# Lightning attention and a routed expert layer on one core: the order of two weight requests, and the form of one step's score products

## The chip, the cores and the metric

The kernel runs on one core of one Trainium2 chip. The metric is the device time of one execution in microseconds (us); the time before is the median of four runs. The profile is that of one more execution, with the start and end of every instruction and the marks that transfers leave when they land.

## The reference

Two stages. The first is a block-wise causal attention with a decay per head; the second sends each token through one of eight experts.

```python
# q, k, v: (4, 8, 768, 64), block of 64, a decay lam per head
for b in range(nb):
    intra = einsum('bhic,bhjc->bhij', qb, kb) * Dmask      # lam**(i-j) for i >= j
    intra = einsum('bhij,bhjd->bhid', intra, vb)
    inter = einsum('bhid,bhde->bhie', qb * lam_pow, kv_state)
    out[:, :, sl] = intra + inter
    kv_state = lam_block * kv_state + einsum('bhsd,bhse->bhde', kb_dec, vb)
# x = out as (4, 768, 512); w_gate (512, 8), w1 (8, 512, 1024), w2 (8, 1024, 512)
for s in range(S):
    fresh_e = argmax(logits[b, s])
    e = fresh_e if s == 0 or local_gate[b, s] < 0.5 else prev_e
    h = maximum(x[b, s] @ w1[e], 0)
    out[b, s] = p[e] * (h @ w2[e])                         # p: softmax of the logits
```

All values are 32-bit floats. The expert of a token depends on the attention's output, so which weights are needed is known only while the kernel runs.

## The kernel before, in words

**Attention.** 24 steps, one for 128 positions of one sequence (`ORDER`, four sequences in turn). A step's input is loaded on SP's queue into one of six buffers. TensorE (PE) multiplies queries by keys (`scores`), VectorE (DVE) multiplies by the decay mask (L212), PE multiplies by the values (`mix`, L248) after the part from the state (`from_state`, L235), updates the state (`update`, L262) and turns the output to rows (`rows_of`, L272), which go to DRAM. `scores(s + 1)` runs ahead of `mix(s)` in steps 0 and from 6 on; in steps 1 to 4 it comes after it, and `scores(6)` comes between `from_state(5)` and `mix(5)`.

**Two forms of the score products.** A step has four pairs of heads, and `u` picks the head of a pair; a head has 64 channels, which are the rows of the product. For the steps in `WIDE` (3, 4, 5, 6) each head is one product of 128 keys by 128 queries (L200): 8 products. For the other steps the keys are cut in two halves of 64, and the second half is multiplied with the second 64 queries only (L208), since later keys are masked for earlier queries: 16 products. Both write the same PSUM banks; what the second form leaves unwritten has a zero in the mask.

**Experts.** While attention ends, the tokens are ranked by expert and cut into tiles of 128 rows of one expert. The first five tiles (0 to 4, `KA` = 5) use the tokens of the first half of the positions. The rest becomes pairs of tiles (two tiles of one expert, multiplied in a scheme of seven products instead of eight, with sums of the weights made on DVE), some whole tiles, and half tiles for what is left (the first of them a quarter tile here). In this run the order is: tiles 0 to 3; tile 4 and the preparation of the first pair; pairs 0 and 1 with three half tiles spread over them as hooks; pair 2; three whole tiles; the rest of the pairs.

**Weights.** There are three sets of buffers, each w1 (first layer) and w2 (second layer), 2 MB each: `w1t[0..2]`, `w2t[0..2]`. Tiles 0 to 3 and 4 alternate between sets 0 and 1. Pair 0 uses set 1, pair 1 set 0, the half tiles set 2. All weight transfers are issued by SP, on one queue, in the order in which the program names them. `weights_of(g, i, layers)` reads the expert of tile `g` into a register and issues the transfers of the layers into set `i` (L685 for w1, L687 for w2). A transfer is issued only when the last reader of its buffer is done, and what stands behind it in SP's order waits too.

**Around the change.** At the end of the first block SP's order is: pair 0's w1 (after tile 3's first layer, since tile 3 uses set 1), the first half tile's w1 and w2 (`G2`; w1 when `by_slots` has read what lay in `w1t[2]`; `w2t[2]` is free), then in the second block the three numbers that choose the branches, and pair 0's w2 (when tile 3's second layer has been multiplied). Next are the second pair's weights, asked for in hook 1 of pair 0 after a copy on DVE (L1204).

In pair 0 DVE makes the sums of w1 (`sums_1`, L935 and L936), adds up products (L993), makes the first sums of w2 (`sums_2`, L937), flips a gathered tile (L717) and adds two more products (L1003, L1004), in this order. PE's product into `c` (bank `po0`, L1011) needs L1004. The half tile's steps run in hooks 7 to 10 of pair 0: turned (L1086), first layer (L1096, reads `w1t[2]`), turned again (L1106), second layer (L1118, reads `w2t[2]`). The weights of the next half tile are asked for when these are done.

Both blocks run under a manual schedule: every engine's order is the program's.

Of the kernel before, what the change touches and what calls it, by code (L numbers as in the profile page):

```python
# [38 lines left out]
PARTS = [(0, 8), (8, NA), (NA, NT)]  # L39
LOADS = 6  # L40
QUARTERS = [16, 17, 18, 19]
WIDE = [3, 4, 5, 6]
WARM = 10
KA = -(-(NA * P - E * (P - 1)) // P)

# [8 lines left out]
G2 = G1 + E  # L54
# [10 lines left out]
def kernel(  # L65
# [26 lines left out]
    def w1_src(e):  # L92
        return w1[bass.ds(e, 1)].rearrange("o (t p) f -> p (o t) f", p=P)

    def w2_src(e):
        return w2[bass.ds(e, 1)].rearrange("o (t p) d -> p (o t) d", p=P)
# [89 lines left out]
    def scores(s):  # L186
# [8 lines left out]

        if s in WIDE:
            for a in range(A):
                for u in range(2):
                    rows = slice(DH * u, DH * u + DH)
                    nc.tensor.matmul(ps[u][:, a], lhsT=kt[rows, a], rhs=qt[rows, a],  # L200
                                     start=True, stop=True, skip_group_check=True)
        for a in range(A if s not in WIDE else 0):
            for j in range(2):
# [434 lines left out]
    def rows_out(i):  # L638

        got = nows["got"]  # L640
        nc.vector.tensor_scalar(got[:, 0], got[:, 0], 0.0, float(SKIP), ALU.is_equal, ALU.mult)
        nc.vector.tensor_tensor(sidx[i], got[:, 0], gidx[i], ALU.add)

    def both_halves():

        twin = pl[:, :5 * (E + 1)].rearrange("p (k g) -> p k g", k=5)
        few = nows["few"]
        nc.tensor.matmul(twin[:, :, :E], lhsT=dupb, rhs=few, start=True, stop=True, skip_group_check=True)
        nc.tensor.matmul(twin[:, :, E:], lhsT=dupq, rhs=few[:, :, 0:1], start=True, stop=True, skip_group_check=True)
        got = act.tile([P, 5, E + 1], F32, name="twin", bufs=1)  # L650
        nc.vector.tensor_copy(got, twin)
        src = act.tile([P, 2, E + 1], F32, name="srch", bufs=1)
        nc.vector.tensor_scalar(src[:, 0], got[:, 0], -float(P), 0.0, ALU.add, ALU.max)
        nc.vector.tensor_scalar(src[:, 1], got[:, 0], 0.0, float(SKIP), ALU.is_equal, ALU.mult)
        nc.vector.tensor_tensor(src[:, 0], src[:, 0], src[:, 1], ALU.add)
        nc.vector.tensor_tensor(src[:, 0], src[:, 0], got[:, 1], ALU.add)
        nc.vector.scalar_tensor_tensor(sidxh[:, :E], src[:, 0, :E], 2.0, upper.broadcast_to([P, E]), ALU.mult, ALU.add)
        nc.vector.scalar_tensor_tensor(sidxh[:, E:], src[:, 0, E:], 4.0, fourth, ALU.mult, ALU.add)
        nc.vector.tensor_tensor(got[:, 2], got[:, 2], got[:, 3], ALU.add)
        nc.vector.tensor_tensor(gateh, got[:, 2], got[:, 4], ALU.add)  # L660
# [7 lines left out]
    def expert(g, own=None):  # L668
        i, j = at(g)
        if own:  # L670
            i = own
        return nc.values_load(owner[i][0:1, j:j + 1], engines=[SP], min_val=0, max_val=E - 1,
                              skip_runtime_bounds_check_because="an index of 8 experts")
# [8 lines left out]
    def weights_of(g, i, layers=(1, 2), cond=None, own=None):  # L682
        e = expert(g, own)
        if 1 in layers:
            nc.sync.dma_start(out=w1t[i], in_=w1_src(e), cond=cond, cond_hint=None if cond is None else True)  # L685
        if 2 in layers:
            nc.sync.dma_start(out=w2t[i], in_=w2_src(e), cond=cond, cond_hint=None if cond is None else True)  # L687

    def w_of(p):
        return (p + 1) % 2  # L690
# [44 lines left out]
    def output(i, w, fs=range(FT)):  # L735
        for f in fs:
            nc.tensor.matmul(pys[i], lhsT=hq[f // 4, i][:, f % 4], rhs=w2t[w][:, f], start=(f == 0), stop=(f == FT - 1))  # L737
# [28 lines left out]
    def number(k, n):  # L766
        return nc.values_load(arms[k][0:1, 0:1], min_val=0, max_val=n - 1,
                              skip_runtime_bounds_check_because="a number of tiles")
# [16 lines left out]
    with tc.manual_schedule(engines={PE, DVE, SP, POOL}):  # L785
# [125 lines left out]
        weights_of(KA, w_of(0), (1,))  # L911
        output(1, 1, range(FT // 2))
        by_slots(1, (0, 1, 2, 3, 4))
        weights_of(G2, 2)
        output(1, 1, range(FT // 2, FT))
        written(3, 1)

# [47 lines left out]
    def pair_ahead(p):  # L965
        for i in range(2):
            ahead(KA + 2 * p + i, i)
# [212 lines left out]
    with tc.manual_schedule(engines={PE, DVE, SP, ACTE}):  # L1180
        more, fulls, halves = (number(k, n) for k, n in enumerate((PMAX - PMIN + 1, E + 1, FIRST_SMALL + 1)))
        weights_of(KA, w_of(0), (2,))
        both_halves()
        pair_ahead(0)
        rows_out(1)
        ahead_half(0)
        sums_1(0, range(3))
        pair_flipped(0)
        pair_flipped(1)
        hidden(0, 0, 0)  # L1190
        hidden(0, 0, 1)
        pair_moved(0, 0)
        moved(xp(0, 1), xqs[1], copy=nc.vector.tensor_copy)
        sums_1(0, (3,))
        output(0, 0)
        sums_of_x(0)
        pair_ahead(1)
        written(4, 0)

        def first_pairs(n, first=2):  # L1200
            hooks = hooks_of_halves(n, first)

            def loads():
                nc.vector.tensor_copy(owner[2], owner[1])  # L1204
                weights_of(KA + 2, w_of(1), own=2)

            hooks.setdefault(1, []).insert(0, loads)
            pair(0, hooks)
            pair(1, {k - 14: f for k, f in hooks.items()})

        def others():
            weights_of(G1, 2)
            rows = [xgh, *xgt]

            def full_ahead(f):
                collect(rows[f % 3], *at(G1 + f))

            pair(2, {0: [lambda: full_ahead(0)], 10: [lambda: full_ahead(1)], 12: [lambda: full_ahead(2)],
                     6: [lambda: flipped(xqs[0], rows[0])], 7: [lambda: moved(xtt[0], xqs[0])]}, load=False, further=False)

            def w_of_full(f):
                return w_of(2) if f % 2 else 2

            def full(f, n=E):

                i, w = f % 2, w_of_full(f)
                if f + 3 < n:
                    full_ahead(f + 3)
                if not f:
                    weights_of(G1 + 1, w_of_full(1), cond=fulls > 1)  # L1230
                if f + 1 < n:
                    flipped(xqs[1 - i], rows[(f + 1) % 3])
                hidden(i, w, 0)
                hidden(i, w, 1)
                if f + 1 < n:
                    moved(xtt[1 - i], xqs[1 - i])
                output(i, w)
                written(G1 + f, i)
                if f + 2 < n:
                    weights_of(G1 + f + 2, w, cond=fulls > f + 2)  # L1240

            def rest(asked=False):
                if not asked:
                    pair_ahead(4)
                weights_of(KA + 8, w_of(4), cond=more > 0)
                rows_of_pair(3)
                pair(3, cond=more > 1, write=False)

                def later_pair(k, last):

                    write_pair(yt)
                    pair(PMIN + k, {11: [lambda: rows_of_pair(PMIN + k)]}, next=not last, load=not last and PMIN + k + 2 < PMAX,
                         cond=more > k + 2, write=False)

                def later_pairs(k):

                    if PMIN + k + 1 == PMAX:
                        return later_pair(k, True)
                    with tc.If(more > k + 1, preferred_fallthrough_block=True) as cmp:
                        later_pair(k, False)  # L1260
                        later_pairs(k + 1)
                    with cmp.Else():
                        later_pair(k, True)

                with tc.If(more > 0, preferred_fallthrough_block=True) as cmp:
                    later_pairs(0)
                with cmp.Else():
                    for i in range(2):
                        nc.vector.tensor_copy(yl[:, i], yt[:, i])

            with tc.If(fulls == 3, preferred_fallthrough_block=True) as cmp:
                for f in range(3):
                    full(f, 3)
                    if f:
                        ahead(KA + 7 + f, f - 1)
                rest(True)
            with cmp.Else():
                while_more(fulls, 0, E, None, full)
                rest()


        with tc.If(halves == FIRST_SMALL, preferred_fallthrough_block=True, label="halves") as cmp:
            first_pairs(3, 4)
            others()
        with cmp.Else():
            one_of(halves, [3, 4, 2, 5, 1, 6, 0, 7, 8], None, first_pairs)
            others()
        write_pair(yl)
# [44 lines left out]
```

## Time and profile before

| what | us |
|---|---|
| four runs | 452.09, 452.58, 453.19, 458.5 |
| their median | 452.88 |
| the profiled execution | 450.47 |
| its span, first to last instruction | 448.7 |
| attention (to the first expert product) | 0 to 100.9 |
| tiles 0 to 4 | 100.9 to 176.6 |
| pairs 0 and 1 with the half tiles | 176.6 to 251.2 |
| pair 2, three whole tiles, the other pairs | 251.2 to 441.5 |

The granted TensorE clock is 0.998 on the mean. Weights and inputs come over the DMA queue q1 (104.62 MB). PE's rate of work in the 40 slices is 9 tenths nearly everywhere.

In the profile a line such as L937 is a line of the kernel; an arrow shows what is written from what is read; "x16" is the number of instructions. A 32-bit product appears as two matmul records, so the 8 products of L200 are 16 records and the 16 of L208 are 32 (some records merge in the views). The chain that ended last is read from the end backwards: each entry was released by the one before it.

The forms of the score products, from the answer for each line:

```profile
L200 PE MATMUL ps<-inp x64: 272/272/373, 15.8 to 28.7; 64*128 64x128 f32 x64
```
```profile
L208 PE MATMUL ps<-inp x608: 213/269/321, 6.5 to 95.6; 64*64 64x128 f32 x116, 64*64 64x64 f32 x36
```

These are times of one record from issue to modelled end in ns; records overlap.

### The profile page before, as it was taken

The page shows a single profiled execution, that of the slowest core. Times are in us where ns is not written, and L with a number is a line of the kernel's source. Part 1 is how long each engine was busy: PE and PEld are TensorE (multiplying, and loading weights), DVE is VectorE, ACT ScalarE, POOL GpSimd, SP SyncE. Part 2 cuts the span into 40 slices and gives each one's busy share as a digit, 9 for nine tenths or more (in the row PEclk, how much of TensorE's full clock was granted, in tenths as well). Part 3 has the DMA queues.
Part 4 walks back from the last instruction along what each step waited for, and adds up shares of the span by engine and source line. Part 5 has one row for each costly group of instructions (what it writes and reads, how often), then busy time and mean ns, then how long its engine had stood idle before and what let it go on. Part 6 is the DMA issues. An engine that isn't in the chain of part 4 may idle for free.

```text
span 448.7 us, 10497 instructions
## 1 busy us (share of the span) xinstructions
PE 432.6 (96%) x4186; PEld 359.3 (80%) x4186; DVE 278.3 (62%) x562; ACT 201.7 (45%) x594; POOL 109.3 (24%) x120
## 2 busy tenths in 40 slices
PE   7999999999999999699999999999999999999993
PEld 6887887778666786688686999677899999898982
DVE  5547777871339959666473796100487888878661
ACT  2356566446455105543534448451445455556110
POOL 4476565321100042103220400210102011020101
PEclk9999999999999999999999999999999999999999
DMA  8999999979899899999993599997153838380101
GB/s 271 408 421 403 317 315 347 383 250 368 304 400 362 277 406 380 355 404 383 380 362 127 172 403 367 349 354 271 43 212 104 309 103 284 138 282 4 53 3 51
DMA packets 42575, 124.85 MB, mean 278 GB/s; under 512 B 3148, under 2 KB 3148, under 8 KB 40592
## 3 DMA queue, kind: packets, MB, share of 16 engines
q1 hardware_dynamic: 34976, 104.62, 63.8%
q0 software_dynamic: 4368, 13.90, 8.9%
q10 hardware_dynamic: 3168, 5.51, 3.3%
q8 instruction: 37, 0.61, 0.5%
q14 instruction: 26, 0.21, 0.2%
HBM read 124.02 MB, written 12.91 MB: 305 GB/s over the span
## 4 chain that ended last, share of the span: by engine, by line
PE 76%; DMA 12%; issue 5%; DVE 4%; POOLq 0%; POOL 0%
PE ps L731 11%; PE pk L962 11%; PE pk L737 11%; PE ps L957 10%; DMA out_dram<-y,sidxp 6%; PE po L248 5%; DMA w<-in_w_dram 5%; PE po L957 5%; PE pl L962 4%; PE ps L208 3%; PE pk L272 3%; PE pk L262 2%; PE pr L1118 2%; PE po L235 2%; PE pr L1096 2%
## 5 line engine op out<-in xcount | busy, mean ns | idle before, releaser
L731 PEld LDWEIGHTS ps<-xt,w 128*128 128x128 f32 x512 | 58.2, 192 | 3.0 <-issue 2.9
L731 PE MATMUL ps<-xt,w 128*128 128x128 f32 x512 | 59.1, 276 | 0.3 <-issue 0.3
L737 PE MATMUL pk<-w,h 128*128 128x512 f32 x128 | 56.5, 593 | 0.0
L737 PEld LDWEIGHTS pk<-w,h 128*128 128x128 f32 x128 | 23.6, 190 | 26.3 <-issue 25.6
L703 POOL DMA_INDIRECT xg<-x_dram,gidx x25 | 25.8, 1032 | 60.5 <-DVE lg L717 39.3
L746 POOL DMA_INDIRECT out_dram<-y,sidx x14 | 14.0, 1002 | 105.8 <-DVE y L763 46.5
L212 DVE TENSOR_TENSOR sm<-ps,mask 128x512 f32<-128x512 f32 x46 | 29.6, 685 | 14.8 <-PE ps L200 7.4
L724 ACT COPY xp<-xlast 32x128 f32<-32x128 f32 x128 | 37.8, 295 | 1.7
L733 ACT ACTIVATE h<-ps 128x512 f32<-128x512 f32 x16 | 9.6, 597 | 57.6 <-PE ps L731 57.6
L724 ACT COPY xp<-lg 32x128 f32<-32x128 f32 x112 | 33.0, 295 | 2.6
L763 DVE TENSOR_SCALAR y<-pk,gate 128x512 f32<-128x512 f32 x8 | 6.0, 744 | 42.1 <-PE pk L737 30.4
L957 PEld LDWEIGHTS ps<-xp,w 128*128 128x128 f32 x256 | 30.5, 192 | 1.7 <-issue 1.3
L957 PE MATMUL ps<-xp,w 128*128 128x128 f32 x256 | 31.3, 275 | 0.0
L957 PE MATMUL ps<-xs,s 128*128 128x128 f32 x256 | 31.2, 275 | 0.0
L177 POOL TENSOR_TENSOR qd<-inp,lamq 128x512 f32<-128x512 f32 x20 | 25.6, 1278 | 22.4 <-PE po L235 10.6
L962 PE MATMUL pk<-w,h 128*128 128x256 f32 x128 | 30.5, 381 | 0.0
L962 PE MATMUL pk<-s,hsum 128*128 128x256 f32 x128 | 30.3, 380 | 0.0
L957 PEld LDWEIGHTS ps<-xs,s 128*128 128x128 f32 x256 | 29.9, 192 | 0.0
L248 PE MATMUL po<-sm,inp 128*64 128x128 f32 x384 | 27.7, 280 | 2.1 <-DVE sm L212 1.2
L248 PEld LDWEIGHTS po<-sm,inp 128*64 128x64 f32 x384 | 20.9, 136 | 9.1 <-issue 6.8
L962 PEld LDWEIGHTS pk<-s,hsum 128*128 128x128 f32 x128 | 23.9, 190 | 3.3 <-DVE s L1045 0.2
L962 PEld LDWEIGHTS pk<-w,h 128*128 128x128 f32 x128 | 23.5, 190 | 3.4 <-issue 0.6
(280 smaller groups left out, 793.1 us busy)
## 6 DMA issues: line engine op xcount, KB each, us to landing
w<-in_w_dram SPq DMA_DIRECT2D x43, 2048.0 KB, 9.9
inp<-in_qkv_dram SPq DMA_DIRECT2D x15, 1024.0 KB, 8.3
x_dram<-xn ACTq DMA_DIRECT2D x21, 256.0 KB, 3.1
inp<-in_qkv_dram SPq DMA_DIRECT2D x10, 512.0 KB, 8.8
inp<-in_qkv_dram SPq DMA_DIRECT2D x4, 768.0 KB, 6.9
w<-in_w_dram SPq DMA_DIRECT2D x4, 512.0 KB, 8.9
x_dram<-xn SPq DMA_DIRECT2D x2, 256.0 KB
xg<-x_dram,gidx POOLq DMA_INDIRECT x25
```

What stands on the lines that cost most here:

```text
L177: nc.gpsimd.tensor_tensor(qd, x[:, 0].rearrange("p (a i) -> p a i", i=P), lamq, ALU.mult)
L208: nc.tensor.matmul(ps[u][half, a, first:], lhsT=kt[rows, a, half], rhs=qt[rows, a, first:], start=True, stop=True, skip_group_check=True)
L212: nc.vector.tensor_tensor(sm[:, u], ps[u], mask[:, u], ALU.mult)
L248: nc.tensor.matmul(head(a, u), lhsT=vn[:, a, u], rhs=sm[:, u, a], start=(not c and a < 2), stop=True, skip_group_check=True)
L272: nc.tensor.transpose(px[:, P * a:P * a + P], xc[:, a, ORDER[s][0]], ident)
L703: nc.gpsimd.indirect_dma_start(out=xg, out_offset=None, in_=x_dram[:n, :], in_offset=bass.IndirectOffsetOnAxis(ap=gidx[i][:, j:j + 1], axi ...
L724: copy(xt[QP * j:QP * j + QP, :, QP * k:QP * k + QP], blocks[QP * k:QP * k + QP, :, j])
L731: nc.tensor.matmul(ph[:, j], lhsT=w1t[w][:, d, P * f:P * f + P], rhs=xtt[i][:, d], start=(d == 0), stop=(d == DT - 1))
L737: nc.tensor.matmul(pys[i], lhsT=hq[f // 4, i][:, f % 4], rhs=w2t[w][:, f], start=(f == 0), stop=(f == FT - 1))
L746: apart(nc.gpsimd.indirect_dma_start(out=out, out_offset=bass.IndirectOffsetOnAxis(ap=sidx[i][:, j:j + 1], axis=0), in_=y, in_offset=None, ...
L957: nc.tensor.matmul(to[:, m], lhsT=a[:, k, P * m:P * m + P], rhs=b[:, k], start=(new and not m and not k), stop=(k == 1), skip_group_check= ...
L962: nc.tensor.matmul(to, lhsT=a[:, f], rhs=b[:, f], start=(new and not f), stop=(f == FT // 2 - 1), skip_group_check=True)
```

## The change

Two edits that do not touch each other. Step 6 leaves `WIDE`, so its scores are made by the 16 products of L208. And the request for the first half tile's two transfers moves from inside tile 3's second layer to behind the request for pair 0's w2, into the second block.

```diff
-WIDE = [3, 4, 5, 6]
+WIDE = [3, 4, 5]
...
         output(1, 1, range(FT // 2))
         by_slots(1, (0, 1, 2, 3, 4))
-        weights_of(G2, 2)
         output(1, 1, range(FT // 2, FT))
         written(3, 1)
...
         weights_of(KA, w_of(0), (2,))
+        weights_of(G2, 2)
         both_halves()
         pair_ahead(0)
```

SP's order becomes: pair 0's w1, the three numbers, pair 0's w2, the half tile's w1 and w2. The orders of DVE, ScalarE (ACT) and GpSimd (POOL) stay as they are; PE's has 8 products more in step 6.

## The prediction

> **What bounds the kernel now.** I read the page first: busy times, the 40 slices, the chain that ended last.
>
> ```profile
> PE 432.6 (96%) x4186; PEld 359.3 (80%) x4186; DVE 278.3 (62%) x562; ACT 201.7 (45%) x594; POOL 109.3 (24%) x120
> ...
> PE   7999999999999999699999999999999999999993
> ...
> PE 76%; DMA 12%; issue 5%; DVE 4%; POOLq 0%; POOL 0%
> ```
>
> PE is busy 96% of the span. One slice inside the run, the seventeenth (179 to 191 us), shows a 6: there PE lies still. I asked for the chain of waits around it, then for PE's own waits over the whole run.
>
> ```profile
> 162.66 0.01 PE pl L649
> 162.67 21.95 DMA w<-in_w_dram
> 184.62 0.02 issue
> 184.64 1.24 DVE s L937
> 185.88 0.02 issue
> 185.90 1.23 DVE w L937
> 187.12 0.62 DVE lg L717
> 187.75 0.58 DVE part L1003
> 188.33 0.02 issue
> 188.35 0.70 DVE part L1004
> 189.05 0.04 issue
> 189.10 2.05 PE po L957 x16
> ```
> ```profile
> PE po L957 <- DVE part L1004: 3.4, 1, 3.4
> ```
>
> The story: the first pair's second-layer weights (w2 of tile 5, the destination w2t[1]) are asked for at 162.67, when the last of the four tiles before it has been multiplied, and land 21.95 us later. Until then DVE stands at its first sum over them (L937, idle 3.40 us). Behind that sum in DVE's order wait a flip and the two additions L1003 and L1004; L1004 frees the bank `po0` that PE's next product writes. So PE stands from 185.72 (183.77 + 1.95, its last product) to 189.10. It is the longest wait of PE in the whole run after its start.
>
> Why 21.95 us? The issue times on SP's queue (the page's DMA queue q1):
>
> ```profile
> 153.77 5.91 SPq L685 DMA_DIRECT2D w<-in_w_dram  x2
> 159.89 6.55 SPq L687 DMA_DIRECT2D w<-in_w_dram  x2
> ```
>
> Four issues, two to a row: w1 of the pair (153.77), w1 of the half tile (159.31), w2 of the half tile (159.89), w2 of the pair (162.67). Each is 2 MB. By the marks that the last of the 16 engines leaves, they landed at 161.9, 170.3, 178.7 and 184.6: in the order asked for, 6 to 8 us apart, while gathers shared the engines. The half tile's pair of transfers stands ahead of the one that is needed first: it reads its w1 at 196.76 (L1096) and its w2 at 202.50 (L1118), 26 and 24 us after they landed.
>
> **Part one: the order of the weights.** No transfer is added or removed; SP issues the pair's w2 at the same moment as now (it still waits for the last L737 matmul), then loads the half tile's expert number and issues w1 and w2. SP passes nothing else: the next entry of its queue, the second pair's weights, waits anyway for a copy on DVE at 181.07 and is issued at 182.21. POOL, ACT and DVE keep their orders.
>
> When does w2 land now? A 2 MB transfer asked for on an all but empty queue took 8.1 us (153.77 to 161.9) or 9.4 (146.63 to 156.0). Three gathers of 256 KB are issued at 160.30 to 162.97; at 410 GB/s that is 1.9 us if w2 must wait for all of them. So 170.8 to 174.0. DVE wants it when its copy L1204 ends, 181.07 + 0.17 = 181.24: at least 7 us to spare. The wait of 3.40 us goes whole.
>
> What is late next? DVE's five instructions then end 3.40 earlier, L1004 at 189.04 - 3.40 = 185.64. PE could start the product at 183.77 + 1.79 = 185.56 (1.79 is the distance of the same two products in the third pair, 258.31 and 260.10). So PE starts near 185.70, held 0.1 us by the same L1004, and gains 189.10 - 185.70 = 3.40 us. From 189 on PE has no gap over 0.1 us to the last product, so the whole tail moves with it, if no transfer is late.
>
> Is one late? The queue now runs dry from 161.9 until w2's first bytes, about 2.5 us later; part of it is filled by the gathers. In return the dry spell of now closes: around 182.5 to 185.0 the last of w2 trickled in and the second pair's weights had only just been asked for (272 GB/s in that stretch against 411 in the next), while in the changed kernel the half tile's w2 is still on its way there. I put the shift of everything behind at 0 to 1 us, at worst the 3.4 us between the asking times 159.31 and 162.67. Against that, with PE 3.4 us earlier:
> - half tile's w1: lands by 178.7 + 3.4 = 182.1, read at 193.4; its w2 by 184.6 + 3.4 = 188.0, read at 199.1. 11 us to spare each.
> - second pair's w1: landed 190.4; DVE reads it at 197.34 - 3.40 = 193.94, and after these sums DVE idles 2.79 us now. 3.5 plus 2.8 us to spare.
> - second half tile's w1: landed 208.1; PE reads it at 213.76 - 3.40 = 210.36. 2.3 us to spare, the tightest; with the worst shift PE would wait 1.1 us.
> - second half tile's w2: landed 212.8, read at 221.56 - 3.40 = 218.2.
>
> So part one: -3.4 us; between -2.3 (worst shift) and -3.4.
>
> [...]
>
> **Part two: the score products of step 6** (the fourth of WIDE). Out go 8 products of 64x128 stationary, in come 16 of 64x64, half of them over 64 queries only. The chain has both forms, on PE, back to back with their neighbours:
>
> ```profile
> 27.92 1.09 PE ps L200 x16
> ...
> 31.09 0.81 PE ps L208 x24
> ```
>
> The difference is 0.28 us. Step 6's scores are this L200 row; PE is busy without a gap from there to 37.1, and every later DVE stretch on the chain (79.35 to 86.1) starts with a wait for PE, so the 0.28 us is passed on. The mask multiply that reads the products starts 0.28 earlier and ends before mix 6 wants it (30.34 against 32.29). The instruction stream grows by 32 entries on PE and 0.5 us pauses without a releaser (0.54 at 37.12, 0.40 before 49.74, 0.52 at 89.12) may fall elsewhere: one more or one less is the bound, -0.82 to +0.26.
>
> [...] The rows above say 0.28 us cheaper, and I go by them.
>
> **The sum.** -3.40 - 0.28 = -3.68 us. The profiled execution took 450.47 (span 448.7, and 1.8 around it): 446.8. The four shown runs have a median of 452.88, 2.4 above it; the same 3.68 makes 449.2, or -0.8%. A measurement of this kernel can tell about 1%, here 4.5 us, from no change: 448.4 is the border.
>
> **Rivals.**
> - *Part of it is given back to a later transfer.* The dry spell moves the whole queue by 3.4 us and the second half tile's w1 keeps PE 1.1 us, a fetch pause of 0.5 us is added: 449.2 + 1.6 = 450.8. For: margin of 2.3 us only. Against: the dry spell of 182.5 closes.
> - *The gain is nil: another input of DVE takes w2's place.* The flip L717 needs a gather (landed 178.5, now wanted at 183.6), the pair's sums need the second pair's w1. Either must be some 8 to 10 us later than now. Then 452.6.
> - *Slower: the second half tile's w1 falls behind more than the spell.* Place: L1096 at 210.4. Each us of landing past it is a us of PE; it decides the sign when it lands after 210.4 + 3.7 = 214.1, that is 6.0 us later than now. Two transfers' spacing (about 13 us) would give 210.4 to 221.1, 10.7 - 3.7 = 7.0 us slower: 459.9. For: SP's queue is in order and the half tile's 4 MB now stand behind a wait. Against: the bytes in the queue are the same, and it is never without work from 165 to 213.
> - *It does not do what it says*: w2 still lands after 181.2. It would have to take over 18.5 us on an empty queue, against 8.1 and 9.4. 452.6.
>
> **How the numbers follow.** Forecast 0.76 (own range 448.1 to 450.3: the pause bound of 0.54 and the 0.55 half spread of the three close runs, 452.09 to 453.19). Part given back 0.10 (450.3 to 452). Nil, by either road, 0.07 (452 to 453.5). Slower 0.07. Low end: 449.2 less all three pauses (1.46) and 0.55 is 447.2. High end: through the second case and half of the nil cases, 452.9. Faster by over 1% means under 448.4: the lower edge of the forecast, 0.24. Slower by over 1% (over 457.4): 0.05. Within: 0.71.
>
> **What would show it.** w2 of the pair lands between 170 and 174; L937 follows L1204 without idle; PE's longest wait after its start is under 1 us and slice seventeen reads 9; the half tile's w1 and w2 land by 188; one L200 row less, a 0.81 us row in its place. Wrong if L1096 or L935 shows a wait on a transfer, or if PE stands at L957 for L1004 again.

## The result, and the profile after

| kernel | runs | median, us |
|---|---|---|
| before | 78 | 452.74 |
| after | 52 | 450.85 |

The ratio is 0.9961 [0.9949, 0.9973]: 1.8 us faster, half of the 3.68 us forecast. Runs more than 1.5% above the fastest of their kernel are left out of the ratios and differences of this document. The profiled execution of after took 452.47 us (span 450.8). That of before, 450.47 us, lies 2.3 us under the median of its kernel. Laid side by side, the two profiles would therefore show a loss of 2 us where the runs show a gain of 1.8, so they have to be compared stretch by stretch. Lines L915 to L1182 have a number one lower in after: L937 becomes L936, L957 L956, L1096 L1095.

From the page of after: busy time of PE, its 40 slices, the instruction queue of part 3, and the chain that ended last.

```profile
PE 433.8 (96%) x4202; PEld 359.6 (80%) x4202; DVE 278.6 (62%) x562; ACT 202.1 (45%) x594; POOL 109.3 (24%) x120
...
PE   7998999889999999999999999999999999999993
...
q8 instruction: 37, 0.61, 0.5%
...
PE 82%; DMA 7%; issue 6%; DVE 2%; POOLq 0%; POOL 0%
```

The 6 in the seventeenth slice is a 9 now, DVE's share of the chain fell from 4% to 2% and that of transfers from 12% to 7%. In return there are 8s in slices four, eight and nine, and "issue" has grown.

SP's queue in the timeline of after (start, duration, line):

```profile
159.24 0.37 SPq L685 DMA_DIRECT2D w<-in_w_dram  x1
168.14 0.37 SPq L687 DMA_DIRECT2D w<-in_w_dram  x1
169.28 0.17 SPq L685 DMA_DIRECT2D w<-in_w_dram  x1
170.02 0.45 SPq L687 DMA_DIRECT2D w<-in_w_dram  x1
```

The order is the new one: pair 0's w1, its w2, then the half tile's two. By the last mark that the trace holds (13 of the 16), the w2 landed at 179.7, that is 11.6 us after it was asked for, where 8 to 11 were forecast. The chain of after around the old gap:

```profile
182.26 3.57 PE ps L956 x32
185.83 1.79 PE po L956 x16
187.62 3.57 PE ps L956 x32
```

PE goes from product to product; no transfer and no DVE instruction stands between them.

Where did the rest go? One mark splits the run in two: the first expert product (L731). PE reached it at 100.92 before and at 106.39 after, 5.47 us later. From there to PE's last instruction it needed 340.54 us before and 337.07 after: 3.47 us less. So part one's 3.40 is there, and the time was lost in the attention phase, which the weights' order does not touch. The timeline of PE, cut to the instructions with an idle time ahead that nothing in the profile explains (in brackets, "issue"), first before, then after:

```profile
37.66 0.33 PE L262 MATMUL pk<-inp,kd 128*64 128x64 f32 x3 [0.54 <-issue]
...
49.74 0.27 PE L248 MATMUL po<-sm,inp 128*64 128x128 f32 x1 [0.40 <-issue]
...
89.64 0.87 PE L248 MATMUL po<-sm,inp 128*64 128x128 f32 x11 [0.52 <-issue]
```
```profile
37.99 0.32 PE L248 MATMUL po<-sm,inp 128*64 128x128 f32 x1 [1.16 <-issue]
...
61.35 0.66 PE L235 MATMUL po<-qd,kv 64*64 64x128 f32 x13 [0.84 <-issue]
...
79.84 0.55 PE L248 MATMUL po<-sm,inp 128*64 128x128 f32 x6 [0.70 <-issue]
...
86.30 0.61 PE L208 MATMUL ps<-inp 64*64 64x64 f32 x18 [0.92 <-issue]
...
92.83 0.43 PE L235 MATMUL po<-qd,kv 64*64 64x128 f32 x3 [1.40 <-issue]
...
97.65 0.67 PE L235 MATMUL po<-qd,kv 64*64 64x128 f32 x12 [0.28 <-issue]
```

Three pauses of 1.46 us in all became six of 5.30 us. In five of the six a packet of the instruction queue q8 (16 KB) had ended 1.3 to 1.5 us before PE went on: at 36.49, 59.81, 78.34, 85.01 and 91.39. Before, all three were like that (packets ended at 36.19, 48.31 and 88.33). Step 6 itself did what was said: in the chain its scores take 0.81 us. But the scores of step 7, the next, took 1.13 instead of 0.81.

```profile
27.89 0.81 PE ps L208 x24
...
30.80 1.13 PE ps L208 x26
```

### The profile page after: what moved, and what is told of

Same layout as the page of the kernel before. It is cut to its first block, busy times and chain, and to the rows that moved or that the text cites. A ratio compares the mean times of both kernels' runs of the same rounds, so it can differ in the third digit from the quotient of the medians.

```text
span 450.8 us, 10529 instructions
## 1 busy us (share of the span) xinstructions
PE 433.8 (96%) x4202; PEld 359.6 (80%) x4202; DVE 278.6 (62%) x562; ACT 202.1 (45%) x594; POOL 109.3 (24%) x120
## 4 chain that ended last, share of the span: by engine, by line
PE 82%; DMA 7%; issue 6%; DVE 2%; POOLq 0%; POOL 0%
PE ps L731 13%; PE pk L737 12%; PE ps L956 12%; PE pk L961 11%; DMA out_dram<-y,sidxp 6%; PE po L248 5%; PE po L956 5%; PE pl L961 4%; PE ps L208 4%; PE pk L272 3%; PE po L235 2%; PE pk L262 2%; PE pr L1117 2%; PE pr L1095 2%; PE pl L286 1%
## 5 line engine op out<-in xcount | busy, mean ns | idle before, releaser
L731 PEld LDWEIGHTS ps<-xt,w 128*128 128x128 f32 x512 | 58.2, 192 | 3.0 <-issue 2.9
L731 PE MATMUL ps<-xt,w 128*128 128x128 f32 x512 | 59.1, 276 | 0.3 <-issue 0.3
L956 PEld LDWEIGHTS ps<-xp,w 128*128 128x128 f32 x256 | 30.4, 192 | 1.7 <-issue 1.3
L956 PE MATMUL ps<-xp,w 128*128 128x128 f32 x256 | 31.3, 275 | 0.0
L956 PE MATMUL ps<-xs,s 128*128 128x128 f32 x256 | 31.2, 275 | 0.0
L956 PEld LDWEIGHTS ps<-xs,s 128*128 128x128 f32 x256 | 29.9, 192 | 0.0
```

Source lines behind the costliest of these rows:

```text
L731: nc.tensor.matmul(ph[:, j], lhsT=w1t[w][:, d, P * f:P * f + P], rhs=xtt[i][:, d], start=(d == 0), stop=(d == DT - 1))
L956: nc.tensor.matmul(to[:, m], lhsT=a[:, k, P * m:P * m + P], rhs=b[:, k], start=(new and not m and not k), stop=(k == 1), skip_group_check= ...
```

## The experiments

A time of one kernel scatters by more than 1 us from run to run. Below, ratios are to the kernel before on the same chip with their 95% interval; differences in us are between mean times of 10 to 33 runs on the same chip, with one standard error in brackets. "Attention" is the time of the first expert product in the one profile of that kernel, "rest" the time from there to PE's last instruction.

| kernel | 128-key steps | order | ratio | attention | rest |
|---|---|---|---|---|---|
| before | 3 to 6 | old | 1 | 100.92 | 340.54 |
| after | 3 to 5 | new | 0.9961 [0.9949, 0.9973] | 106.39 | 337.07 |
| f1, after again | 3 to 5 | new | 0.9942 [0.9913, 0.9971] | 103.08 | 336.93 |
| g2, after again | 3 to 5 | new | 0.9947 [0.9915, 0.9979] | 104.28 | 337.23 |
| e1 | 3 to 6 | new | 0.9913 [0.9881, 0.9945] | 104.15 | 337.17 |
| g1, e1 again | 3 to 6 | new | 0.99 [0.9871, 0.9928] | 103.59 | 337.18 |
| e2 | 3 to 5 | old | 1.0016 [0.9986, 1.0047] | 103.11 | 339.19 |
| e3, before and products | 3 to 6 | old | 1.0006 [0.998, 1.0032] | 103.42 | 341.06 |
| f2, e1 and products | 3 to 6 | new | 0.9925 [0.9893, 0.9958] | 102.69 | 337.91 |
| e4 | 2 to 5 | new | 0.9907 [0.988, 0.9933] | 102.67 | 336.92 |
| f3 | 2 to 6 | new | 0.9946 [0.992, 0.9971] | 99.56 | 340.54 |
| f4 | 3, 4 | new | 0.9936 [0.9907, 0.9966] | 105.59 | 337.09 |
| g3, before, PE later | 3 to 6 | old | 1.0019 [0.9987, 1.0051] | 104.96 | 340.86 |
| g4, e1, PE later | 3 to 6 | new | 0.9969 [0.9939, 0.9998] | 105.32 | 337.15 |

### Each part by itself

Order alone, with `WIDE` as before; run twice, on two chips:

```diff
...
         by_slots(1, (0, 1, 2, 3, 4))
-        weights_of(G2, 2)
...
         weights_of(KA, w_of(0), (2,))
+        weights_of(G2, 2)
```

> Only the requests are moved; step 6 keeps its 8 products of 128 keys. In the two profiles the part from the first expert product to the end became 3.5 us shorter (100.9 to 448.7 before, 106.4 to 450.8 after), and attention 5.5 us longer, with more pauses of PE that nothing releases. [...] Theory 'the order gains less' (the profiles of single executions mislead): -1.5 to -2 us, 0.996 to 0.997, as the whole change.

> The order alone, beside the changed kernel on one chip (the first comparison of the two was on different chips). If step 6's small products cost 1 to 2 us: 0.991 to 0.9925, and the next run 0.995 to 0.997. If they save 0.28 us as forecast: both within 0.2% of each other, this one the slower.

Measured: 448.33 and 449.47 us at the median; by the means 3.5 and 3.9 us faster than before (0.45 each). Part one alone brings what was forecast of it, and more than the whole change.

'Place' and 'rate' in what was expected are suppositions on PE's pauses that no run shows: that it matters where the borders of q8's 16 KB packets fall in PE's stream, and that step 6's 16 products use up instructions faster than they arrive. The other part alone:

```diff
-WIDE = [3, 4, 5, 6]
+WIDE = [3, 4, 5]
```

> Only step 6 gets the 16 products of 64 keys; the requests stay as before. 'Place' and 'rate': +1.5 to +2 us, 1.0033 to 1.0045, with the loss between 28 us and the first expert product. 'The order gains less', and the forecast: -0.28 us, 0.9994.

Measured: 453.33 us, +0.9 (0.5): no gain. PE's waits in this kernel have the old gap, in another size than before's 3.4:

```profile
PE po L957 <- DVE part L1004: 2.2, 1, 2.2
```

Attention ended 2.19 us later than in the profile of before and the pair's w2 was asked for 2.19 us later (164.86), but it landed only 1.0 us later (185.6): 20.73 us after the asking, not 21.95. The gap is shorter by about as much as PE's lateness exceeds that of the landing, 1.2 us.

The changed kernel itself, again on two chips:

> The changed kernel itself, beside the next three on one chip. If step 6's small products cost what the first runs say, it stands 2 us above the order alone (which was 0.9913): 0.995 to 0.997. If that was a difference between chips: 0.991 to 0.993.

> The changed kernel, beside the order alone. Cost of 1 to 2 us: 0.995 to 0.997. Saving of 0.28 us: within 0.2% of the order alone, a little faster.

Measured: 449.31 and 450.35 us, 3.1 and 2.5 us faster than before (0.5 each). On the chip where both ran, the changed kernel (450.38 us on the mean) was 1.4 us (0.5) slower than order alone (448.97). So the second part takes back something; the first profile of after, with its late first expert product, overstates how much.

### Is it the number of instructions, or where they fall?

Two theories for the pauses, both suppositions: *count* (PE's stream has 32 more records, 16 matmuls and 16 weight loads: x4202 of each against x4186; they would be brought over q8 while the loads use the DMA engines) and *place* (the stream behind step 6 is shifted, and with it the points at which the next 16 KB would be needed). The first test puts 32 small records after the first scores and leaves all products alone, in the old order (e3) and in the new (f2):

```diff
...
+            if not s:
+                for _ in range(8):
+                    nc.tensor.matmul(warm[:EP, 0, :1], lhsT=ident[:, :EP], rhs=ident[:, :1], start=True, stop=True)
```

> The kernel before, with 8 tiny products (one column each, result unread) put on PE between the first two score products and the first mix, where PE waits 1 us for the mask. [...] 'Place': +1.5 to +2.3 us, 1.003 to 1.005. 'Rate': 0 to +0.3 us, under 1.001. 'The order gains less': the same as 'rate'.

> [...] 'Place' (the borders decide): 0.995 to 0.997, like the changed kernel. 'Count' (what decides is how many instructions PE must be brought while the loads keep the DMA engines full; the tiny ones are run in a gap): 0.990 to 0.9925, like the order alone.

Measured for e3: 452.18 us, +0.2 (0.45), where *place* had at least 1.5. For f2: 448.54 us; its interval holds both the ratio of order alone and that of the changed kernel, so this one decides nothing. In f2's profile PE waits 0.92 us at the second half tile's first layer:

```profile
213.04 3.65 PE L1098 MATMUL pr<-w,xth 128*64 128x512 f32 x16 [0.92 <-DVE part L995]
```

The view names a DVE instruction, which ended at 212.91. The last mark of the w1 that L1098 reads came at 212.90; and in e4's profile, below, PE began the same product 0.86 us before the same DVE instruction ended, so it was the weights that it waited for.

Which steps, and how many:

```diff
-WIDE = [3, 4, 5, 6]
+WIDE = [2, 3, 4, 5]
```

> [...] 'Place': -3.4 to -3.7 us, as with the order alone, 0.992 to 0.9925. 'Rate': -1.5 to -2 us, 0.996 to 0.997, as the whole change. 'The order gains less': -1.5 to -2 us too.

> The new order, 128-key products in five steps, 2 to 6. 'Count': 32 instructions fewer than with four, so 1 to 2 us better than the order alone, 0.987 to 0.990. 'Place': another set of borders, anything between 0.988 and 0.997. If instructions cost nothing but their own time: 0.28 us above the order alone, 0.992.

> The new order, 128-key products in two steps, 3 and 4: 32 instructions more than the changed kernel. 'Count': 1 to 2 us worse than the changed kernel, 0.998 to 1.001. 'Place': between 0.988 and 0.997. If instructions cost nothing but their own time: 0.28 us better than the changed kernel.

f3 has `[2, 3, 4, 5, 6]` and f4 `[3, 4]`, all three in the new order. Measured: 447.25, 450.19 and 449.55 us. e4 is the fastest kernel of all, though not distinct from order alone (-1.0, with an error of 0.5, on one chip). It has step 6 in the small form, as after has, and as many products as order alone: so the form of step 6 by itself is not what costs. *Count* does not come out everywhere: f3 was to be 1 to 2 us faster than order alone, and f4 as much slower than the changed kernel, which it is by 0.4 us (0.6). By the profiles attention ended at 99.56 with five such steps, at 100.92 to 104.15 with four, at 103.08 to 106.39 with three, at 105.59 with two (g3 and g4, which have other products ahead of that mark, left aside). f3's only two pauses in the same list as above:

```profile
43.51 0.44 PE L235 MATMUL po<-qd,kv 64*64 64x128 f32 x5 [0.18 <-issue]
...
82.64 0.43 PE L235 MATMUL po<-qd,kv 64*64 64x128 f32 x2 [0.43 <-issue]
```

Its attention ended earliest of all, and yet by the ratios it is 1.5 to 2 us behind order alone. Its chain and its PE timeline say where:

```profile
193.93 16.05 DMA w<-in_w_dram
```
```profile
210.12 3.65 PE L1095 MATMUL pr<-w,xth 128*64 128x512 f32 x16 [1.13 <-DMA w<-in_w_dram]
```

PE reached the second half tile's first layer before its w1, which landed at 210.0. In e4 PE read the same w1 at 212.03 and it had landed at 211.6: it passed by 0.5 us. An early attention alone does not explain it: counted from the asking of the pair's w2, PE came to this product after 47.6 to 47.7 us in all ten profiles of the new order, and the w1 landed after 46.9 to 48.7 us, latest in f3 (48.7) and f2 (48.5). f2's attention ended when e4's did, at 102.7, and e4's w1 took 47.1. Why the landing varies stays open. In f3's profile a further pause of 2.0 us without a releaser stands at 415.95 (L956); a q8 packet had ended 1.3 us before. These two places make up most of f3's longer rest; whether they are there in most of its runs isn't shown.

Attention by itself: four kernels that end after the last of the 24 steps, with four, three, five (2 to 6) and four steps and the small products.

```diff
...
-            if s == NS - 1:
-                nc.sync.dma_start(out=w1t[1], in_=w1_src(1))
-                nc.sync.dma_start(out=w2t[1], in_=w2_src(1))
...
+        rows_of(NS - 1)
+        nc.sync.dma_start(out=out[0:P, :], in_=xlast)
...
+        return
```

> Attention alone: the kernel before, cut off after the last step's rows; the expert layer, the last two weight requests of attention and all output but one block of rows are left out. 128-key products in steps 3 to 6. Its time, about 110 us, is what the next three are compared with; the ratio to the whole kernel says nothing.

> The same cut, with the changed kernel's steps 3, 4, 5. 'Count' (PE waits for its instructions while the loads fill the DMA engines, so 32 more of them cost more than the products save): 1 to 2 us above the first. 'Place': 1 to 2 us above it too. As forecast: 0.28 us below it.

> The same cut, steps 2 to 6. 'Count': 1 to 3 us below the first (one profile of this choice had the first expert product at 99.6 us, against 100.9 to 104.2 with four steps). 'Place': anything within 2 us of the first. If instructions cost nothing but their own time: 0.28 us above the first.

> [...] 'Place': as the second, 1 to 2 us above the first. 'Count': 0 to 0.5 us above the first, since the extra instructions are used up in a gap of PE, before the loads fill the engines. If instructions cost nothing: 0.

| kernel | runs | median, us | mean of all, us | mean of the fastest, us (runs) |
|---|---|---|---|---|
| h1, four steps | 7 | 111.94 | 111.5 | 109.8 (3) |
| h2, three | 6 | 113.30 | 112.8 | 111.2 (2) |
| h3, five | 6 | 110.23 | 110.6 | 109.4 (3) |
| h4, four and the products | 6 | 112.16 | 111.9 | 111.2 (3) |

Either way five steps are fastest, then four, then three; three is 1.4 us (0.8) above four. What the added products cost depends on the column: 0.45 (0.7) by all runs, nearer to *count*, but 1.4 (0.3) by the fastest, as late as h2, which is what *place* had. So these runs do not separate the two theories.

The pauses of all the profiles side by side say more than any one of them. Their sum over attention was 0.6 us with five 128-key steps (f3), 1.5 to 4.5 with four (3.4 on the mean of before, e1, g1, e4, g3 and g4), 3.9 and 4.2 with four and the small products (e3, f2), 4.5 to 5.3 with three (4.7 on the mean of after, e2, f1 and g2) and 5.0 with two (f4). And 63 of these 65 pauses end 1.0 to 1.7 us after a 16 KB packet of q8, although such packets come only every 6.0 us on the mean of before's attention and every 6.2 us of after's.

### Does the gap swallow time?

e2 raised the question whether anything that delays attention is free in the old order. Fifteen products more ahead of the first expert product delay PE after the attention phase, in the old order and in the new:

```diff
...
+        for _ in range(15):
+            nc.tensor.matmul(pys[0][:, :P], lhsT=ident, rhs=ident, start=True, stop=True)
         hidden(0, 0, 0)
```

> The kernel before with 15 products of 128 by 128 (result unread) on PE ahead of the first expert product: the expert layer starts about 3 us later. Theory 'elastic wait' (the wait for the pair's w2 is set by the DMA queue, so it shrinks when PE comes later, as in the profiles of step 6 alone and of the pad, where it was 2.2 us instead of 3.4): +1 to +2 us, 1.002 to 1.0045, and PE's wait at the third product of the pair 1 to 2 us in the profile. Theory 'fixed wait' (as in the forecast, the 3.4 us are there in every run): +3 us, 1.0066.

> The order alone with the same 15 products. Both theories: no wait is left that could take them up, so +2.5 to +3 us above the order alone. Then the two orders differ by less when the expert layer starts late: 'elastic wait' 1.5 to 2.5 us, 'fixed wait' as much as without the delay.

Measured: +1.6 (0.5) on before, +2.3 (0.5) on order alone. The difference, 0.7 us with an error of 0.7, cannot tell the theories apart. The profiles speak against a wait that goes on shrinking: the gap in g3 is 2.1 us, as in e2 and e3, though attention ended between 103.1 and 105.0 in these three, and w2 took 20.7 us in each. Only the profile of before, with its early attention, has 3.37.

### The clock behind the gap

e3's profile showed one thing that the profile of before did not. Windows of it: length, busy time of PE, PEld, DVE, ACT and POOL, then the granted clock, the share of the DMA engines and GB/s.

```profile
190.00:192.00 2.00, 1.62 (x13) 1.62 (x14) 1.97 (x3) 1.12 (x2) 0.31 (x1) 0.91 1.00 401
192.00:194.00 2.00, 2.00 (x11) 2.00 (x11) 1.40 (x2) 0.15 (x1) 0.00 (x0) 0.50 1.01 354
194.00:196.00 2.00, 2.00 (x14) 1.98 (x14) 1.46 (x3) 0.48 (x1) 0.00 (x0) 0.73 1.03 399
```

```profile
190.38 2.65 PE L960 MATMUL po<-xs,w 128*128 128x128 f32 x16 [2.16 <-DVE part L1007]
```

After a gap of 2.16 us (PE went on at 190.38) the clock is at half from 191.65 for 3.41 us, and a group of 16 product records that takes 1.95 us elsewhere took 2.65. In g3's profile the clock is at half from 192.8, and the same 16 records took 2.87 us; e2's has 1.00 from 186 to 198. So has the profile of before around its gap of 3.37 us, in the same columns:

```profile
185.00:187.50 2.50, 0.72 (x7) 0.53 (x5) 2.47 (x3) 0.00 (x0) 0.00 (x0) 1.00 1.01 411
187.50:190.00 2.50, 0.90 (x8) 0.90 (x9) 2.47 (x4) 0.86 (x2) 1.01 (x1) 1.00 1.04 396
190.00:192.50 2.50, 2.50 (x25) 2.50 (x24) 2.00 (x3) 0.62 (x2) 0.00 (x0) 1.00 1.01 377
```

Since every run lists its mean clock, this can be counted: one such window is half of 3.41 us in 450, 0.0038 of the mean. (At the very end the clock is at half too, from 446.72 in before and from 446.22 in after, behind PE's last product, which ended at 441.46 and 443.46, so it costs PE nothing there; that alone puts the means of these two profiles at 0.998 and 0.995. The other profiles have 0.994 to 0.998, but for e3, g3 and f4, each with a further window: 0.992, 0.992 and 0.991.) Of the runs of before, 50 to 62% have a mean below 0.9935 on the three chips of these kernels, and they took 0.8 to 2.3 us longer than the others; of the 21 runs of order alone, none has. The mean clock is 0.9919 to 0.9926 before and 0.9957 to 0.9967 with order alone.

The other kernels of the new order are not free of it: 15 of the 78 runs listed for the changed kernel are below 0.9935, 3 of 12 of f3, 4 of 12 of f4, and none of 11 of e4. There the gap is gone, so such a window must have another place; f4's profile has one in attention (last section). For the changed kernel, 15 of 78 at 1.9 us is some 0.4 us, which may be a part of what step 6 costs.

## Why the forecast was off

**Part one: right, in mechanism and size, but not made up as I thought.** I took 3.40 us from one gap in one profile. Order alone gained 3.5 and 3.9, and rest fell from 340.5 to 337.2 between the profiles of before and of order alone. But the gap is 2.1 to 2.2 us in three of the four profiles of the old order, and by the mean clocks such a gap was followed by a window of half clock in about half of the runs. e3's rest is 341.06 with the window and e2's 339.19 without, 1.87 apart, which at half the runs is some 0.9 us. The two sum to 3.1 of a measured 3.7 (0.3); the missing 0.6 us stays open.

**The clock: a term that was missing.** The forecast has none for it. In the profile of before the clock is 1.00 from 185.0 to 192.5, and the products of L957 take 275 ns at the median after the gap as before it. The profiles of e3 and g3 have the half clock behind gaps of 2.16 and 2.13 us, and e3's rest is 1.87 us longer than that of e2, whose clock is 1.00 there. One profiled execution could not show a thing that happens in half of the runs. This error was hidden in the sum by luck, since the gap was oversized by about as much.

**Part two: the step that failed the forecast.** "-0.28", bounded at "-0.82 to +0.26" by one pause more or less. Three comparisons say a loss: e2 against before +0.9 (0.5), g2 against g1 +1.4 (0.5), h2 against h1 +1.4 (0.8); weighted, +1.2 (0.3). The products were priced rightly, 0.81 instead of 1.09. The pauses were not: I let one of 0.54 come or go, from a profile that happened to have three short ones. After has six of up to 1.40 us, but e1 has five of 4.4 us in all and g1 six of 4.5, with the four steps of before. So the pauses change from run to run by far more than my bound, and single profiles don't resolve a mean of 1 us. The means over the profiles do so roughly: 3.4 us with four 128-key steps, 4.7 with three. 1.4 us (0.5) more of pauses less the 0.28 saved is 1.1, near the loss that was measured. So the step that failed is that 32 records more were taken to cost nothing but their own time, give or take one pause. That the stream's feeding is what PE pauses for is inferred from the q8 packets, since no run changes the feeding alone. Whether the pauses follow the number of instructions, or where they fall too, is not settled: the pad of e3 cost little, that of h4 1.4 us by the fastest runs, and f4 is no slower than the changed kernel within its error. And a part of the 1.2 us can be clock, as said above.

I went by the rows of the two forms alone, and for the products they held. In the total the 16 small products were dearer, and the loss is in the pauses, 63 of 65 of which end 1.0 to 1.7 us after a 16 KB packet of q8.

**The point of departure.** I set -3.68 on the median of the runs, with terms from a profile that was 2.3 us faster than it: fewer pauses, no window of half clock ahead of PE's last product. What such an execution waits for is not what a typical one waits for.

**What is late next.** I put the shift of the weights behind at 0 to 1 us. Counted from the asking of the pair's w2 to the landing of the second half tile's w1, it was 45.5 us before and 46.9 to 48.7 in the profiles of the new order: 1.5 to 3.2 more, up to nearly the worst case that I had named. PE came after 47.6, as forecast. The tightest margin, 2.3 us, was thus 0.1 to 0.7 in eight of these profiles, after's among them, and gone in f2 and f3. The rival "part of it is given back to a later transfer" named the right place, and f3 shows its price, 1.13 us where I had 1.1. Its 450.8 is also what was measured for the changed kernel, but by luck: in none of the three profiles of that kernel did PE wait for this transfer, and the pauses cost more than the 0.5 us that the rival gives them. The half tile's w2 landed 24.7 us after the asking of the pair's w2 (192.8 less 168.14), where 188.0 less 162.67, 25.3, was forecast. The other rivals did not occur.

In sum: -3.7 for the order and +1.2 for step 6 give -2.5; the changed kernel measured -1.8 (by the ratio), -3.1 and -2.5.

## What to carry to other kernels

Order transfers by first use, and then look up every later transfer of that queue, since what was gained is lost at the first one with no margin, as in f3's profile, where PE waited 1.13 us for it. Never price an edit of some tenths of a microsecond from one profile: take the same kernel's profiles of several experiments side by side, split the run at a mark that the edit does not touch, and test each part by itself. An idle gap of TensorE is worth more than its length where the clock falls behind it, as after e3's gap of 2.16 us: 16 records took 2.65 us there instead of 1.95.

## What was not expected of the hardware

- A gap of 2.16 us was followed by a half clock of 3.41 us in e3's profile, and one of 3.37 us by none in that of before. A pause inside attention was followed by one as well: in f4 PE went on at 78.99 after 1.63 us without a releaser, and the stretch from 80 to 84 has a clock of 0.58.

```profile
78.99 0.43 PE L235 MATMUL po<-qd,kv 64*64 64x128 f32 x3 [1.63 <-issue]
```
```profile
80.00:84.00 4.00, 4.00 (x57) 3.71 (x60) 2.42 (x10) 1.05 (x3) 0.82 (x1) 0.58 0.78 273
```

- Pauses of up to 1.7 us without a releaser, two to seven in the 100 us of attention, 63 of 65 of them ending 1.0 to 1.7 us after a 16 KB packet of the instruction queue. With four 128-key steps their sum was 1.46 us in before, 4.37 in e1, 4.49 in g1 and 3.64 in e4: they differ by more from one profile to the next than the edit that was to be priced.
